# One Trainium2 core, sorted attention then four experts: early expert weights spread by GpSimd, and the head's first steps dealt to two engines

## The chip, the cores and the metric

The kernel runs on one core of a Trainium2 chip. Five engines work side by side, each with its own in-order queue: TensorE (PE; its weight loads are listed as PEld), VectorE (DVE), ScalarE (ACT), GpSimd (POOL) and SyncE (SP, which here only issues transfers). Sixteen DMA engines serve several queues. The metric is device time in microseconds (us) of one execution; the median over the runs counts.

## What is computed

```python
# attention: B, H, S, D = 4, 8, 768, 64; 8 blocks of 96 tokens
P = sort_net                                   # (B, H, 8, 8)
for _ in range(5):                             # Sinkhorn
    P = exp(P - max(P, -1)); P /= sum(P, -1) + 1e-9; P /= sum(P, -2) + 1e-9
k_sorted = einsum('bhij,bhjcd->bhicd', P, k_blocks)      # blocks mixed by P
v_sorted = einsum('bhij,bhjcd->bhicd', P, v_blocks)
attn = softmax(q_blocks @ k_sorted^T / sqrt(D))          # within each block of 96
x = (attn @ v_sorted), heads joined                      # (3072, 512)
# experts: E = 4, F = 1024
p = domain_probs / (sum(domain_probs, -1) + 1e-9)        # (3072, 4)
out = sum over e of p[:, e:e+1] * (relu(x @ w1[e]) @ w2[e])
```

Inputs are float32; the matrix products run in float16 with float32 sums.

## The kernel before

The order of the work on every engine is written out by hand: an engine runs its instructions in the order of the program text, and semaphores make it wait where it reads or overwrites what another engine has not yet finished. The expert products use a scheme of seven half-size products per block pair, so weights and hidden values are first added and subtracted (`weight_sums`, `h_sums`).

**The head (0 to some 19 us).** `sn` (32 heads by 8 by 8) is loaded, and five Sinkhorn rounds alternate between ACT (exp) and DVE. PE meanwhile multiplies a dummy block (`warm`). In the last round the column factor is multiplied in while `sn` is widened to `sn16` (L330): DVE writes the first four of the eight rows i, GpSimd the other four. `r_half(0)` (L342) multiplies `sn16` by the identity so that each factor stands on 128 partitions in PSUM (`ps_R`); `build_PI0` (L353) multiplies this by a mask and gives `PI0[0]`, the mixing matrices of the first four blocks, on DVE in two pieces of four heads. Heads are handled in two quads (`qd`), blocks in two halves (`hf`). `mix_half` (L521) mixes k or v of one quad on PE; `mixed` (L532) copies a range of blocks from PSUM; `h_w` (L548) transposes v and copies it (L553); `h_s` (L576) makes scores, with exp on ACT (L582); `h_a` (L593) applies them to v, DVE normalises (L606, L607); `h_x` (L624) transposes the result into `xT`, the experts' input, using `perm`; `group0` (L704) is the first layer of expert 0. `keep_warm` (L507) puts dummy products where PE waits. The Rs copy (L1402) takes the mixing factors of both halves out of `ps_R`. In the program the first steps stand so:

```python
mk0 = mix_half("k", 0, 0, psm, 8)       # 8 dummy products first
mixed("k", 0, mk0, 0, 2, act)
mv0 = mix_half("v", 0, 0, psa)
mixed("v", 0, mv0, 0, 2, vec)
r_half(1)
act(Rs..., Rv...)
h_s(0, 0)
mixed("k", 0, mk0, 2, 2, act)
```

Later in the head follow `mk1` and `mv1`, the mixes of the second quad. `psm` hands out two PSUM buffers in turn, so a mix waits until the buffer of two mixes before has been copied out.

**Loads.** Queries, k, v and all expert weights are float32 in DRAM and are written as float16 into SBUF; GpSimd issues these transfers, up to eight in flight, and waits for the one eight before (L113, L126, L139, L146, L183, L1456, L1475). SP issues the rest: `sn`, the probabilities twice (`p_in` at L170, with 24 tokens on each partition, and `p_own` at L171, the first 768 tokens one per partition in 16-byte pieces), the stores, and the expert weights' way: DVE divides (`spread_weights`, four steps between the Sinkhorn rounds and one later), SP writes p to DRAM (`p_dram`, L256 and L258), and `load_p` (L230) reads rows of 256 values back to all 128 partitions, as `pb`: DVE multiplies the first layer's result by `pb` where it applies the relu (L821). `load_p_one` (L241) does it for one expert of the second chunk, ahead of time. `own_weights` (L263 to L266) makes `p_sb`, the weight of expert 0 per token, which L748 uses.

**After the head.** `second_layer0` (L741, L748) is the second layer of expert 0 over batch 0; between its parts stand stages of attention (`next_stages`: `h_q_both` L288/L301, `h_w`, `h_s`, `h_a`, `h_x`). `chunk_first` (L815, L821) is the first layer of further experts in chunks of 256 tokens, `chunk` the products of the second layer (L799, L860). Batches 1 to 3 follow by a table of stages (`st_v`, `st_k`, `st_s`, `st_a`; `builds(1)` on GpSimd, L364 and L372, makes batch 1's mixing matrices), and the last five chunks use the seven-product scheme in both layers (L1153, L1166, L1296).

Of the kernel before, what the change touches and what calls it, by code (L numbers as in the profile page):

```python
# [2 lines left out]

# [7 lines left out]
F32 = mybir.dt.float32  # L11
# [7 lines left out]
def kernel(  # L19
# [67 lines left out]
    def from_spare(n):  # L87
        at = spare["at"]
        spare["at"] += n
        return Sflat[:, ds(at, n)]  # L90
# [77 lines left out]
    p_own = p_part(2 * E * NT + NT, R * E).rearrange("p (t e) -> p t e", e=E)  # L168
    own_den = p_part(2 * E * NT + NT + R * E, R).rearrange("p (t o) -> p t o", o=1)
    nc.sync.dma_start(p_in, moe_domain_probs.rearrange("(p t) e -> p t e", t=NT))  # L170
    nc.sync.dma_start(p_own, moe_domain_probs[0:S].rearrange("(t p) e -> p t e", p=P))  # L171
    load_half_queries(0)
    load_natural(0, "k", 0)

# [6 lines left out]
    for kc in range(0, NKC, 2):  # L181
# [15 lines left out]
    )  # L197

    perm = const.tile([BLK, BLK], F16, name="perm")
    nc.gpsimd.tensor_copy(  # L200
        perm.rearrange("p (c r) -> p c r", r=R), ident[0:BLK, 0:BLK].rearrange("p (r c) -> p c r", c=CP)
    )
    kTs, ETs, vs0s, wide = [], [], [], []
    for n in range(2):
        kT = const.tile([P, S + 32], F16, name=f"kT_{n}")
        nc.gpsimd.memset(kT[:, ds(S, 32)], 0.0)
        kTs.append(kT)
    for n in range(4):
        ET = const.tile([P, S + 32], F16, name=f"ET_{n}")
        nc.gpsimd.memset(ET[0:BLK, ds(S, 32)], 0.0)  # L210
        ETs.append(ET[0:BLK])
        wide.append(ET)
    for n in range(2):
        vs0 = from_spare(HB * 4 * VW)[0:BLK].rearrange("c (i s h w) -> c i s h w", i=HB, s=2, h=2)
        nc.gpsimd.memset(vs0[:, :, :, :, ds(D, 2)], 1.0)
        vs0s.append(vs0)
    vo = arena[:, ds(4 * NW + NQ + 4 * 4 * P, R * 4 * VW)].rearrange("p (r h w) -> p r h w", r=R, h=4)


# [3 lines left out]

    pbs = {}

    def load_p(b, c, es=range(E), pb=None):
        if pb is None:
            pb = moe.tile([P, E, 2 * P], F32, name=f"pb_{b}_{c}", tag="pb", bufs=1)
        n = len(es)
        nc.sync.dma_start(  # L230
            pb[:, ds(es[0], n)],
            p_dram[ds(es[0], n), ds(b * S + 2 * c * P, 2 * P)].rearrange("(o e) x -> o e x", o=1).broadcast_to(
                [P, n, 2 * P]
            ),
        )
        return pb

    def load_p_one(b, c, e):

        pb = Tt[3].rearrange("p a f x -> p (a f x)")[:, 0:4 * P].bitcast(F32)  # L240
        nc.sync.dma_start(pb, p_dram[ds(e, 1), ds(b * S + 2 * c * P, 2 * P)].broadcast_to([P, 2 * P]))  # L241
        return pb

    def spread_weights():

        nc.vector.tensor_reduce(p_den, p_in, AX.X, ALU.add)
        yield
        nc.vector.tensor_scalar(out=p_den, in0=p_den, scalar1=1e-9, scalar2=None, op0=ALU.add)
        yield
        nc.vector.reciprocal(p_den, p_den)  # L250
        yield
        nc.vector.tensor_tensor(
            p_out.rearrange("p e t -> p t e"), p_in, p_den.broadcast_to([P, NT, E]), ALU.mult
        )
        p_rows = p_dram.rearrange("e (p t) -> p e t", t=NT)
        nc.sync.dma_start(p_rows[0:S_P], p_out[0:S_P])  # L256
        pbs[(0, 0)] = load_p(0, 0)
        nc.sync.dma_start(p_rows[S_P:P], p_out[S_P:P])  # L258
        yield

    def own_weights():

        nc.vector.tensor_reduce(own_den, p_own, AX.X, ALU.add)  # L263
        nc.vector.tensor_scalar(out=own_den, in0=own_den, scalar1=1e-9, scalar2=None, op0=ALU.add)
        nc.vector.reciprocal(own_den, own_den)
        nc.vector.tensor_tensor(p_sb[:], p_own[:, :, 0:1], own_den, ALU.mult)  # L266
# [59 lines left out]
            if it:  # L326
                next(p_steps)

    for a, eng in enumerate((nc.vector, nc.gpsimd)):
        eng.tensor_tensor(  # L330
            sn16[:, ds(a * HB, HB)],
            sn[:, ds(a * HB, HB)].rearrange("g i (j o) -> g i j o", o=1).broadcast_to([GH, HB, NB, CP]),
            scol[:].rearrange("g j (i o) -> g i j o", i=1).broadcast_to([GH, HB, NB, CP]),
            ALU.mult,
        )

    ps_R = psM.tile([P, 2, 512], F32, tag="ps", name="ps_R")
    Rv = ps_R[:, :, 0:HB * GH].rearrange("p a (i g) -> p a i g", g=GH)
# [13 lines left out]
    def build_PI0(eng, a, h0, hn, src):  # L352
        eng.tensor_tensor(  # L353
            PI0[a][:, ds(h0, hn)],
            maskk[:, 0:HB * CP].rearrange("p (o i c) -> p o i c", o=1, c=CP).broadcast_to([P, hn, HB, CP]),
            src.rearrange("p g (i o) -> p g i o", o=1).broadcast_to([P, hn, HB, CP]),
            ALU.mult,
        )
# [18 lines left out]
            )  # L377

    r_half(0)
    for h0 in range(0, H, 4):  # L380
        build_PI0(nc.vector, 0, h0, 4, Rv[:, 0, :, ds(h0, 4)].rearrange("p i g -> p g i"))
    vec, act = nc.vector.tensor_copy, nc.scalar.copy


# [126 lines left out]
    def mix_half(nm, qd, hf, pool, warm_up=0):  # L511

        ps = pool([P, 1024], F32, f"ps_m{nm}_{qd}_{hf}")
        keep_warm(ps[:, 0:P], warm_up)
        tails[(nm, qd, hf)] = ps[:, 2 * R * 64:1024].bitcast(F16).rearrange("p (n x) -> p n x", n=2)
        ps = ps[:, 0:2 * R * 64].rearrange("p (s r x) -> p s r x", s=2, r=R)
        for sg in range(2):
            for r in range(R):
                for hh in range(2):
                    h = 4 * qd + 2 * sg + hh  # L520
                    nc.tensor.matmul(  # L521
                        ps[ds(D * hh, D), sg, r, :],
                        head(0, nm, h)[:, r, :],
                        PI0[hf][:, h, :, :].rearrange("p i c -> p (i c)"),
                        start=True, stop=True,
                    )
        return ps

    def mixed(nm, qd, ps, i0, n, copy):

        dst = kTs[qd][:, 0:S] if nm == "k" else vT0[qd]
        copy(  # L532
            dst.rearrange("p (i x c) -> p x i c", i=HB, c=CP)[:, :, ds(i0, n)],
            ps.rearrange("p s r (i c) -> p (s r) i c", c=CP)[:, :, ds(i0, n)],
        )
# [4 lines left out]
    def h_v(qd, hf, copy, pool=psa):  # L540
        mixed("v", qd, mix_half("v", qd, hf, pool), 0, HB, copy)
# [24 lines left out]
    def h_s(qd, qq, ps=None):  # L566

        kT, ET = kTs[qd], ETs[2 * qd + qq % 2]
        if ps is None:
            ps = psa([P, 2, 512], F32, f"ps_s0_{qd}_{qq}")  # L570
        for n in range(4):
            for hh in range(2):
                sg, i = n // 2, 2 * (qq % 2) + n % 2

                m = BLK if 2 * i + sg == 3 else P
                nc.tensor.matmul(  # L576
                    ps[0:m, hh, ds(n * BLK, BLK)],
                    kT[ds(D * hh, D), ds((2 * i + sg) * BLK, m)],
                    qT0[qd][ds(D * hh, D), sg, qq // 2, :, ds((2 * (qq % 2) + n % 2) * CP, CP)],
                    start=True, stop=True,  # L580
                )
        nc.scalar.activation(  # L582
            ET[:, 0:S].rearrange("c (h x) -> c h x", h=2), ps[0:BLK, :, 0:HS],
            AF.Exp, bias=0.0, scale=SCALE,
        )
# [248 lines left out]
    def chunk(b, c, slot, done=()):  # L834
# [9 lines left out]
                h_sums(e, 2)  # L844
        nxt = (b, c + 1) if c + 1 < R // 2 else (b + 1, 0)
        first = int(nxt[0] == 0)
        pbs[nxt] = load_p(*nxt, range(first, first + 1))
        rest = lambda: load_p(*nxt, range(first + 1, E), pbs[nxt])
        late = b == c == 1
        if not late:  # L850
            rest()

        blk = lambda kh, tok: (lambda e, f: Hb[:, homes.get(e, e), kh * KH + f, ds(tok * P, P)])
        sm = lambda n: (lambda e, f: Sb[:, n, e, ds(f * P, P)])
# [539 lines left out]
    ]  # L1394


    mk0 = mix_half("k", 0, 0, psm, 8)
    mixed("k", 0, mk0, 0, 2, act)
    mv0 = mix_half("v", 0, 0, psa)
    mixed("v", 0, mv0, 0, 2, vec)  # L1400
    r_half(1)
    act(Rs.rearrange("p g (a i) -> p a g i", a=2), Rv.rearrange("p a i g -> p a g i"))  # L1402
    h_s(0, 0)
    mixed("k", 0, mk0, 2, 2, act)
    load_half_queries(1)
    load_w2(0, 2)
    build_PI0(nc.gpsimd, 1, 0, H, Rs[:, 0:H, HB:NB])
# [24 lines left out]
    even01()  # L1432
    w11(vec)
    group0(0, 1, 1, [0, 1])
    own_weights()
    ps_s11 = ps_a10
    h_s(1, 1, ps_s11)
    evacuate00 = group0(0, 1, 0, [2, 3], True)
# [9 lines left out]
    group0(1, 1, 0, [2, 3])  # L1448
    h_v(0, 1, vec)
    h_v(1, 1, vec)  # L1450
    group0(1, 1, 1, [2, 3])


# [15 lines left out]
            build_PI(nc.gpsimd, n, "k")  # L1469

    load_w2(1)
    load_w2(2)
    load_w1(3)
    def load_w2_part(e, d):
# [22 lines left out]
                f(*args)  # L1497

    second_layer0(0, next_stages)
    load_queries(1, range(2))  # L1500
    load_natural(1, "v", 0, 2, lambda: load_w2_part(3, DH))
    load_natural(1, "k", 0, 2)
    load_natural(1, "v", 1)
    load_natural(1, "k", 1)
    chunk_first(0, 0, [1, 2], 1, next_stages)
    pb_1 = load_p_one(0, 1, 1)
    h_sums(1, 4)
    for w in range(1, 5):
        h_sums(2, w)
# [3 lines left out]
    second_layer0(1, lambda: next(sums2, None))  # L1513
    sums0 = weight_sums(0, nc.vector)
    homes[1] = 0
    chunk_first(0, 1, [1], 1, next_stages, lambda e: pb_1.rearrange("p (o x) -> p o x", o=1))
    homes.clear()


# [27 lines left out]
    for g in range(G0 + 1, GN, 2):  # L1547
        last_second(g, last_first(g))
        last_second(g + 1, upper=True)
# [1 line left out]
_INS = ['q', 'k', 'v', 'sort_net', 'moe_domain_probs', 'moe_w1', 'moe_w2']  # L1551
_OUTS = [((3072, 512), 'float32')]
# [25 lines left out]
```

## Time and profile before

| | |
|---|---|
| median of 3 runs | 358.14 us (358.12 to 358.28) |
| the profiled execution | 358.21 us |
| its span, first to last instruction | 356.3 us |
| PE, DVE, ACT, POOL busy | 350.4, 277.5, 170.1, 137.6 us |
| moved by DMA | 40.26 MB in 74762 packets |
| granted TensorE clock | 1.00 throughout |

The profiled execution is one of the program's; what it takes beside its span (1.9 us) lies before the first and after the last instruction. A row of a group names the line, the engine, the operation, what is written and read, and the busy time; in the chain, each row is a start, a length and what ran. A busy PE is not PE at its peak, since products overlap.

### The profile page before, as it was taken

The numbers are of one execution on the slowest core, as the hardware profiler recorded it, in microseconds if no ns is written. First come the engines' busy times: TensorE is split into PE (matmuls) and PEld (weight loads), VectorE is DVE, ScalarE is ACT, GpSimd is POOL, SyncE is SP. The second block draws the span as 40 slices with busy tenths as digits, with TensorE's granted clock in tenths as the row PEclk, the third lists the DMA queues.
The fourth block names the chain that finished last, engine by engine and source line by source line (L and its number), as shares of the span: only waits on it lengthen the run. The fifth ranks groups of instructions, "written<-read, shape, count | busy, mean of one in ns | idle before, by whom it ended". The sixth has DMA issues, their size and how long they took to land.

```text
span 356.3 us, 9511 instructions
## 1 busy us (share of the span) xinstructions
PE 350.4 (98%) x3948; PEld 305.5 (86%) x3948; DVE 277.5 (78%) x555; ACT 170.1 (48%) x302; POOL 137.6 (39%) x154
## 2 busy tenths in 40 slices
PE   8899999999999999999999999999999999999996
PEld 8686857888888888988899888888888888888886
DVE  5766787779798687778879988896678886588963
ACT  2653330452425445368847259830288611598301
POOL 8766112466022420000626318840068800188400
PEclk9999999999999999999999999999999999999999
DMA  8999999999999999743995410005200014100021
GB/s 104 203 205 230 212 209 194 207 195 167 195 180 166 195 116 203 138 88 44 180 205 91 107 74 0 2 1 136 78 26 3 2 37 141 62 0 2 0 75 46
DMA packets 74762, 40.26 MB, mean 113 GB/s; under 512 B 41568, under 2 KB 70496, under 8 KB 74720
## 3 DMA queue, kind: packets, MB, share of 16 engines
q0 software_dynamic: 38720, 19.93, 43.2%
q1 hardware_dynamic: 35856, 19.67, 27.2%
q8 instruction: 31, 0.51, 0.6%
q14 instruction: 11, 0.09, 0.1%
q10 hardware_dynamic: 144, 0.07, 0.1%
HBM read 41.88 MB, written 6.34 MB: 135 GB/s over the span
## 4 chain that ended last, share of the span: by engine, by line
PE 95%; DVE 3%; issue 0%; DMA 0%; ACT 0%; DVEq 0%
PE ps_h L815 18%; PE ps_Q L1296 18%; PE ps_p L799 12%; PE ps_X L1153 10%; PE ps_Z L1153 7%; PE ps_Q L1153 7%; PE ps_Z L1296 6%; PE ps_h L704 3%; PE ps_o L741 3%; PE ps_p L860 3%; PE ps_a L479 2%; PE ps_s L444 2%; PE ps_k L425 1%; PE ps_v L391 1%; PE ps_mv L521 1%; PE ps_a L593 0%
## 5 line engine op out<-in xcount | busy, mean ns | idle before, releaser
L815 PE MATMUL ps_h<-xT,w 128*128 128x256 f16 x576 | 67.5, 273 | 0.0
L815 PEld LDWEIGHTS <-w 128*128 128x128 f16 x576 | 55.2, 98 | 7.3
L821 DVE SCALAR_TENSOR_TENSOR Hb<-ps_h,pb 128x1024 f16<-128x1024 f32 x34 | 41.5, 1223 | 17.8 <-PE ps_h L815 17.6
L1153 PEld LDWEIGHTS <-w 128*128 128x128 f16 x480 | 43.6, 98 | 4.7
L1166 POOL TENSOR_TENSOR arena<-tmp,pb 128x512 f16<-128x512 f32 x12 | 15.2, 1276 | 65.7 <-PE ps_Z L1153 49.8
L1296 PEld LDWEIGHTS <-Hb 128*128 128x128 f16 x320 | 31.1, 98 | 3.5
L1165 ACT ACTIVATE tmp<-tmp 128x512 f32<-128x512 f32 x46 | 29.0, 632 | 3.9 <-DVE tmp L1203 3.9
L1296 PEld LDWEIGHTS <-Sb 128*128 128x128 f16 x304 | 28.2, 98 | 3.0
L1153 PEld LDWEIGHTS <-arena 128*128 128x128 f16 x312 | 27.7, 98 | 2.8
L451 ACT ACTIVATE ET<-ps_s 96x768 f16<-96x768 f32 x24 | 18.1, 802 | 25.2 <-PE ps_s L444 25.0
L434 ACT CAST kT<-ps_k 64x384 f16<-64x384 f32 x48 | 22.7, 473 | 13.3 <-PE ps_k L425 12.3
L126 POOL DMA_DIRECT2D arena<-in_q_dram x24 | 19.9, 842 | 20.8 <-DMA q_ring<-arena 17.7
L1153 PE MATMUL ps_X<-ET,arena 128*128 128x256 f16 x168 | 25.2, 272 | 0.0
L1296 PE MATMUL ps_Q<-w,Hb 128*128 128x256 f16 x192 | 24.6, 273 | 0.0
L799 PEld LDWEIGHTS <-Hb 128*128 128x128 f16 x232 | 21.9, 98 | 3.0
L1159 DVE SCALAR_TENSOR_TENSOR Hb<-ps_X,pb 128x512 f16<-128x512 f32 x27 | 18.7, 692 | 7.0 <-PE ps_X L1153 7.0
L1173 ACT COPY ps_X<-ps_Z 128x512 f32<-128x512 f32 x27 | 15.4, 571 | 17.8 <-PE ps_Z L1153 17.8
L1153 PE MATMUL ps_Z<-xT,w 128*128 128x256 f16 (+1 forms) x176 | 22.5, 258 | 0.0
L785 DVE TENSOR_TENSOR Sb<-Hb 128x512 f16<-128x512 f16 x33 | 20.6, 646 | 0.0
L1180 ACT COPY tmp<-ps_X 128x512 f32<-128x512 f32 x26 | 15.2, 586 | 9.2 <-PE ps_X L1153 6.6
L1159 DVE SCALAR_TENSOR_TENSOR Hb<-ps_Z,pb 128x512 f16<-128x512 f32 x27 | 18.4, 683 | 1.3 <-PE ps_Z L1153 1.3
L1203 DVE TENSOR_TENSOR tmp<-ps_Q,tmp 128x512 f32<-128x512 f32 x26 | 17.7, 683 | 0.8 <-PE ps_Q L1153 0.8
(270 smaller groups left out, 744.3 us busy)
## 6 DMA issues: line engine op xcount, KB each, us to landing
w<-in_moe_w_dram POOLq DMA_DIRECT2D x4, 1024.0 KB, 27.2
w<-in_moe_w_dram POOLq DMA_DIRECT2D x6, 512.0 KB, 19.7
arena<-in_k_dram POOLq DMA_DIRECT2D x7, 384.0 KB, 7.6
arena<-in_v_dram POOLq DMA_DIRECT2D x7, 384.0 KB, 8.1
vs<-arena SPq DMA_DIRECT2D x36, 66.0 KB, 5.3
arena<-in_q_dram POOLq DMA_DIRECT2D x24, 96.0 KB, 7.5
out_dram<-ob SPq DMA_DIRECT2D x9, 256.0 KB, 2.0
pb<-p_dram SPq DMA_DIRECT2D x4, 512.0 KB, 5.8
```

Of the source, the lines that this page charges most:

```text
L126: nc.gpsimd.dma_start(t[:, h // 2, :, h % 2, :], q[b, h].rearrange("(t p) d -> p t d", p=P))
L434: nc.scalar.copy(kT[ds(D * hh, D), r], pk[ds(D * r, D), hh].rearrange("p a (i c) -> p a i c", c=CP),)
L451: nc.scalar.activation(ETs[2 * (pr % 2) + hh][:, 0:S].rearrange("c (a x) -> c a x", a=2), pss[hh][0:BLK, :, 0:HS], AF.Exp, bias=0.0, scale ...
L785: tt(sm[0], blk(0, 1), blk(1, 1), ALU.add)
L799: nc.tensor.matmul(ps, lhs(e, f), Ts[e][rhs][:, f, :], start=(first and e == es[0] and f == 0), stop=(done and e == es[-1] and f == KH - 1 ...
L815: nc.tensor.matmul(ps[:, f, :], w1sb[e][:, kc, ds((4 * g + f) * P, P)], xT[:, kc, ds(2 * c * P, 2 * P)], start=(kc == 0), stop=(kc == NKC ...
L821: nc.vector.scalar_tensor_tensor(out=Hb[:, homes.get(e, e), ds(4 * g, 4), :], in0=ps[:], scalar=0.0, op0=ALU.max, in1=weights(e).broadcast ...
L1153: nc.tensor.matmul(dst[:, ds(f * cols, cols)], a[lhs][:, k, ds((f0 + f) * P, P)], t[rhs][:, k, :], start=(first and f == 0 and k == 0), st ...
L1159: nc.vector.scalar_tensor_tensor(out=home(i, j), in0=src.rearrange("p (f x) -> p f x", f=m), scalar=0.0, op0=ALU.max, in1=weight(j).broadc ...
L1165: nc.scalar.activation(src, src, AF.Relu, bias=0.0, scale=1.0)
L1203: tt(t12, Q, u2, ALU.add)
L1296: nc.tensor.matmul(ps, lhs(e, f), Ts[e][rhs][:, f, part], start=(first and e == 0 and f == 0), stop=(e == E - 1 and f == KH - 1), skip_gro ...
```

## The change

It has two parts.

*Expert weights of the first two chunks.* For the first chunk SP now loads only the rows of experts 1 to 3 into partition 0 of the tile (`load_rows`), and GpSimd copies partition 0 to all partitions (`spread`, a `partition_broadcast`). That operation needs another library of GpSimd code, loaded in the program after `load_w2(1)`; the usual one is loaded again at the end. `load_p_one` does the same for its row and stands earlier. The second chunk's tile is loaded for experts 2 and 3 only. `p_own` is loaded after p's first write to DRAM, and `own_weights` stands later, after the last mix of v (`h_v(1, 1, vec)`).

*The head.* Row 3 of `sn16` moves from DVE to GpSimd. `PI0[0]` is built in three pieces. The first two blocks of k and of v are copied one by ACT and one by DVE, and k's other two in two pieces. `h_s(0, 0)` stands ahead of `r_half(1)`, the Rs copy moves to DVE, four dummy products go, and the constants (`perm`, zeros, ones) are written by GpSimd after its part of `sn16`.

```diff
-    nc.sync.dma_start(p_own, moe_domain_probs[0:S].rearrange("(t p) e -> p t e", p=P))
     load_half_queries(0)
...
+    def fill_constants():
+        for kT in kTs:
+            nc.gpsimd.memset(kT[:, ds(S, 32)], 0.0)
+        for ET in ETs:
+            nc.gpsimd.memset(ET[:, ds(S, 32)], 0.0)
+        for vs0 in vs0s:
+            nc.gpsimd.memset(vs0[:, :, :, :, ds(D, 2)], 1.0)
+        nc.gpsimd.tensor_copy(
+            perm.rearrange("p (c r) -> p c r", r=R), ident[0:BLK, 0:BLK].rearrange("p (r c) -> p c r", c=CP)
+        )
...
     def load_p_one(b, c, e):
         pb = Tt[3].rearrange("p a f x -> p (a f x)")[:, 0:4 * P].bitcast(F32)
-        nc.sync.dma_start(pb, p_dram[ds(e, 1), ds(b * S + 2 * c * P, 2 * P)].broadcast_to([P, 2 * P]))
+        pb = pb.rearrange("p (o x) -> p o x", o=1)
+        load_rows(pb, b, c, [e])
+        spread(pb)
         return pb
+
+    def load_rows(dst, b, c, es):
+        nc.sync.dma_start(
+            dst[0:1], p_dram[ds(es[0], len(es)), ds(b * S + 2 * c * P, 2 * P)].rearrange("(o e) x -> o e x", o=1)
+        )
+
+    def spread(dst):
+        nc.gpsimd.partition_broadcast(dst, dst[0:1])
...
         nc.sync.dma_start(p_rows[0:S_P], p_out[0:S_P])
-        pbs[(0, 0)] = load_p(0, 0)
+        nc.sync.dma_start(p_own, moe_domain_probs[0:S].rearrange("(t p) e -> p t e", p=P))
+        pbs[(0, 0)] = pb_tile(0, 0)
+        load_rows(pbs[(0, 0)][:, 1:E], 0, 0, range(1, E))
         nc.sync.dma_start(p_rows[S_P:P], p_out[S_P:P])
...
-    for a, eng in enumerate((nc.vector, nc.gpsimd)):
+    for eng, i0, n in ((nc.vector, 0, HB - 1), (nc.gpsimd, HB - 1, 1), (nc.gpsimd, HB, HB)):
         eng.tensor_tensor(
...
+    fill_constants()
...
-    for h0 in range(0, H, 4):
-        build_PI0(nc.vector, 0, h0, 4, Rv[:, 0, :, ds(h0, 4)].rearrange("p i g -> p g i"))
+    for h0, n in ((0, 2), (2, 2), (4, 4)):
+        build_PI0(nc.vector, 0, h0, n, Rv[:, 0, :, ds(h0, n)].rearrange("p i g -> p g i"))
...
-        pbs[nxt] = load_p(*nxt, range(first, first + 1))
-        rest = lambda: load_p(*nxt, range(first + 1, E), pbs[nxt])
         late = b == c == 1
-        if not late:
-            rest()
+        if nxt == (0, 1):
+            pbs[nxt] = load_p(*nxt, range(2, E))
+        else:
+            pbs[nxt] = load_p(*nxt, range(first, first + 1))
+            rest = lambda: load_p(*nxt, range(first + 1, E), pbs[nxt])
+            if not late:
+                rest()
...
-    mk0 = mix_half("k", 0, 0, psm, 8)
-    mixed("k", 0, mk0, 0, 2, act)
+    mk0 = mix_half("k", 0, 0, psm, 4)
+    mixed("k", 0, mk0, 0, 1, act)
+    mixed("k", 0, mk0, 1, 1, vec)
     mv0 = mix_half("v", 0, 0, psa)
-    mixed("v", 0, mv0, 0, 2, vec)
+    mixed("v", 0, mv0, 0, 1, vec)
+    mixed("v", 0, mv0, 1, 1, act)
+    h_s(0, 0)
     r_half(1)
-    act(Rs.rearrange("p g (a i) -> p a g i", a=2), Rv.rearrange("p a i g -> p a g i"))
-    h_s(0, 0)
-    mixed("k", 0, mk0, 2, 2, act)
+    vec(Rs.rearrange("p g (a i) -> p a g i", a=2), Rv.rearrange("p a i g -> p a g i"))
+    for i in (2, 3):
+        mixed("k", 0, mk0, i, 1, act)
...
     group0(0, 1, 1, [0, 1])
-    own_weights()
...
     h_v(1, 1, vec)
+    own_weights()
     group0(1, 1, 1, [2, 3])
...
     load_w2(1)
+    nc.gpsimd.load_library(library_config.all_libraries[10])
+    spread(pbs[(0, 0)][:, 1:E])
     load_w2(2)
...
     second_layer0(0, next_stages)
+    pb_1 = load_p_one(0, 1, 1)
     load_queries(1, range(2))
...
     chunk_first(0, 0, [1, 2], 1, next_stages)
-    pb_1 = load_p_one(0, 1, 1)
...
+    nc.gpsimd.load_library(library_config.standard)
```

More of the change, by code (lines that the diff above doesn't have):

```diff
@@ L5 @@
 import concourse.tile as tile
-from concourse import mybir
+from concourse import library_config, mybir
 from concourse.bass import ds
@@ L199 @@
     perm = const.tile([BLK, BLK], F16, name="perm")
-    nc.gpsimd.tensor_copy(
-        perm.rearrange("p (c r) -> p c r", r=R), ident[0:BLK, 0:BLK].rearrange("p (r c) -> p c r", c=CP)
-    )
     kTs, ETs, vs0s, wide = [], [], [], []
     for n in range(2):
-        kT = const.tile([P, S + 32], F16, name=f"kT_{n}")
-        nc.gpsimd.memset(kT[:, ds(S, 32)], 0.0)
-        kTs.append(kT)
+        kTs.append(const.tile([P, S + 32], F16, name=f"kT_{n}"))
     for n in range(4):
         ET = const.tile([P, S + 32], F16, name=f"ET_{n}")
-        nc.gpsimd.memset(ET[0:BLK, ds(S, 32)], 0.0)
         ETs.append(ET[0:BLK])
@@ L213 @@
     for n in range(2):
-        vs0 = from_spare(HB * 4 * VW)[0:BLK].rearrange("c (i s h w) -> c i s h w", i=HB, s=2, h=2)
-        nc.gpsimd.memset(vs0[:, :, :, :, ds(D, 2)], 1.0)
-        vs0s.append(vs0)
+        vs0s.append(from_spare(HB * 4 * VW)[0:BLK].rearrange("c (i s h w) -> c i s h w", i=HB, s=2, h=2))
+    def fill_constants():
[8 more added lines that the diff above has]
+        )
     vo = arena[:, ds(4 * NW + NQ + 4 * 4 * P, R * 4 * VW)].rearrange("p (r h w) -> p r h w", r=R, h=4)
@@ L224, with pb_tile @@
     pbs = {}
+    def pb_tile(b, c):
+        return moe.tile([P, E, 2 * P], F32, name=f"pb_{b}_{c}", tag="pb", bufs=1)
     def load_p(b, c, es=range(E), pb=None):
         if pb is None:
-            pb = moe.tile([P, E, 2 * P], F32, name=f"pb_{b}_{c}", tag="pb", bufs=1)
+            pb = pb_tile(b, c)
         n = len(es)
@@ L327 @@
                 next(p_steps)
-    for a, eng in enumerate((nc.vector, nc.gpsimd)):
+    for eng, i0, n in ((nc.vector, 0, HB - 1), (nc.gpsimd, HB - 1, 1), (nc.gpsimd, HB, HB)):
         eng.tensor_tensor(
-            sn16[:, ds(a * HB, HB)],
-            sn[:, ds(a * HB, HB)].rearrange("g i (j o) -> g i j o", o=1).broadcast_to([GH, HB, NB, CP]),
-            scol[:].rearrange("g j (i o) -> g i j o", i=1).broadcast_to([GH, HB, NB, CP]),
+            sn16[:, ds(i0, n)],
+            sn[:, ds(i0, n)].rearrange("g i (j o) -> g i j o", o=1).broadcast_to([GH, n, NB, CP]),
+            scol[:].rearrange("g j (i o) -> g i j o", i=1).broadcast_to([GH, n, NB, CP]),
             ALU.mult,
         )
+    fill_constants()
     ps_R = psM.tile([P, 2, 512], F32, tag="ps", name="ps_R")
@@ L1515 @@
     homes[1] = 0
-    chunk_first(0, 1, [1], 1, next_stages, lambda e: pb_1.rearrange("p (o x) -> p o x", o=1))
+    chunk_first(0, 1, [1], 1, next_stages, lambda e: pb_1)
     homes.clear()
```

## The prediction

> **What bounds the kernel now.** I read the page first (busy shares, chain), then the chain in order of time, the table by stage, the timeline of the head, and the landing times of single transfers.
>
> ```profile
> PE 350.4 (98%) x3948; PEld 305.5 (86%) x3948; DVE 277.5 (78%) x555; ACT 170.1 (48%) x302; POOL 137.6 (39%) x154
> ...
> PE 95%; DVE 3%; issue 0%; DMA 0%; ACT 0%; DVEq 0%
> ```
>
> TensorE carries 95% of the chain that ends last, DMA none of it. In the table by stage PE is busy for 7.00 of 7.00 us in 24:31 and 99.97 of 100.00 in 80:180, so later stages have nothing to give. What can be gained lies before 18.8 us; what can be lost lies wherever a cover ends.
>
> The head, from the chain between 16.1 and 18.9 us:
>
> ```profile
> 16.08 0.13 PE ps_s L576 x6
> 16.21 0.52 PE ps_mv L521 x24
> 16.73 0.02 issue
> 16.76 0.57 DVE Sb L532
> 17.32 0.04 issue
> 17.37 0.44 PE ps_mv L548 x4
> 17.81 0.03 issue
> 17.83 0.02 DVEq L553
> 17.86 0.04 issue
> 17.90 0.43 DVE Sb L553
> 18.33 0.04 issue
> 18.37 0.40 PE ps_a L593 x8
> 18.77 0.17 PE ps_h L704 x2
> ```
>
> Here PE and DVE hand work to each other; from 18.77 the first layer fills PE. This last hand-over starts with mixing the second quad's v (`mv1`). The timeline shows when that v arrives:
>
> ```profile
> 16.15 0.57 PE L521 MATMUL ps_mv<-Sb,arena 128*64 128x64 f16 x24
> ...
> 16.39 0.75 POOL L146 DMA_DIRECT2D w<-in_moe_w_dram  x1 [1.18 <-DMA arena<-in_v_dram]
> ```
>
> ```profile
> L113 POOL DMA_DIRECT2D arena<-in_v_dram x1: 760/760/760, 5.6 to 5.6; - x1
> ...
> DMA to landing us min/median/max: 10.5/10.5/10.5
> ```
>
> Issued at 5.62 with 10.5 us to land: v is there at 16.1, `mv1` starts at 16.15. An earlier ready head meets that gate.
>
> **The change, part by part.** The profiled execution took 358.21 us, its span 356.3, so 1.9 us lie around it; the median of the runs is 358.14. I sum against 358.21 and move the result by -0.07.
>
> *Head.* Fits from rows: DVE 0.16 us + 1.04 ns a column (L532: 0.557 us for 384, 0.958 for 768); ACT 0.14 + 0.88 (0.479 and 0.817); Pool's two-input f32 0.16 + 2.2 (0.72 for 256 at L970, 1.27 for 512 at L1166).
>
> - sn16: DVE writes 384 columns, not 512: 0.68 to 0.55. Pool's single row is 0.44 and can start at 10.87, since perm and the memsets (10.44 to 11.27) move behind it: ready at 11.31, DVE at 11.41. Gain 0.13.
> - PI0: the first piece is two heads, 0.29 for 0.42. Gain 0.13; pieces two and three (another 0.6) run behind PE's first twelve matmuls. Four fewer warming matmuls (8 in 0.55) make room; the four removed were cover only.
> - k halves: one piece each on ACT (0.31) and DVE (0.36) in parallel for 0.48 in one. v halves likewise: DVE's piece 0.36 for 0.56. Before, v's first half was ready at 13.99; now mk ends at 12.77, mv at 13.14, DVE's k piece at 13.15, its v piece at 13.53. Gain up to there 0.46.
> - h_s(0,0) goes ahead of r_half(1) on PE, and the Rs copy from ACT (0.37) to DVE (0.16 + 256 x 1.04 ns = 0.42). It falls at 13.75 to 14.17, in DVE's wait for the transposes (0.59 idle before L553); queued behind it are L553 and `mk1`, which needs the PSUM buffer that Rs frees (14.23 instead of 14.40). ACT pays one fixed part more for k's last two pieces and ends `mk1`'s copy at 15.68 for 15.85; that frees `mv1`'s buffer.
> - So PE could start `mv1` at 15.73. But v lands at 16.10. Of the 0.42 nothing comes through unless v lands sooner. What could bring it: p_own's load (768 pieces of 16 bytes, 1.66 to 5.57) leaves this stretch. It is one of the small HW-queue loads beside two query loads that had landed by 6.4, while k and v followed until 16.1 at some 200 GB/s. Bounds for v: 0 to 0.5 us sooner; I take 0.1, since the transfers that it ran beside are not the ones that end last. Head: -0.1 us (0 to -0.42).
> - A moved constant: the ones, zeros and perm (0.83 us on Pool) now end at 13.3; their readers start at 14.6 (h_a), 15.4 (h_s(0,1)), 16.2 (h_x). Half-queries 1 are issued at 13.3 for 12.40; needed at 28.7, landed at 23.2. Nothing.
>
> The row that could undo the 0.13: DVE and Pool now work on sn16 at the same time. Before, they overlap from 11.23 to 11.54 and Pool's op takes 1.23 us, no more than L1166's 1.27 for as many columns. But at 331 us three L785 sums (0.41 each when Pool is quiet) take 3.02 us beside L1166. The Trainium skill (SBUF — State Buffer, section "SBUF: two separate sides") says that a DVE op with two SBUF inputs and a GpSimd op that reads SBUF lock each other out for the whole instruction. The trace agrees at 331 us and does not at 11.2 us. By the rule the row would be ready at 11.85, v's half at 13.96, `mv1` at 16.2, and the sum would be 358.2 instead of 358.0.
>
> *Expert weights.* Removed from the DMA engines: four rows to 128 partitions (512 KB, 25.5 to 35.9), one row (128 KB, 26.6 to 39.2) and two of the four rows at 63.8 (256 KB). 640 KB at some 205 GB/s: the weights behind them land 3.1 us sooner. PE waited for none of them (DMA 0%): 0 us, but a reserve.
> Added on SP, in order: the first write of p (19.99), p_own, the rows (after the write, landed at 25.5), the second write, the one row. On Pool: a library load at 22.6 (w2(1)'s issue ends at 22.59), a broadcast of 768 words and one of 256. Queued behind the first: w2(2), w1(3), half of w2(3), four builds, batch 1's loads; DVE's L821 waits for it. Its own length: nearest is a Pool copy (maskv, 0.30 us for 128 columns; so 1.0), at most L1166's pace (1.9); 1.0. The rows: 3.5 to 5.5 us after 25.5, as the small write took (5.5): 30 to 31. The library load is in no row. From below ACT's table load, 1.28 us; from above, if it waits for the transfers in flight, w2(1)'s landing (21.7 + 25.1 = 46.8). Nearest are SP's transfers of that stretch, 5.5 to 12.6 us to land: Pool free at 28 to 35, broadcast done by 31.5 to 36.2.
> Needed by: L821 starts at 38.79, and with two PSUM buffers PE first waits at 41.16, so it may start at 39.9. Cover 3.7 us or more. The software queue stays fed by w2(1) until 43.7 (46.8 less 3.1), so late issues of w2(2) and after cost nothing. The builds end near 41 and are used at 63.7. The second broadcast's row lands near 33 and holds up nothing that isn't in that queue anyway. Later Pool products run from the other library; taken at the same 1.27 us. The closing reload follows Pool's last op (333.8), 22 us before the end. 0 us.
> The Trainium skill (GPSIMD Engine Reference, 2.1 Instruction dispatch) gives about 6 us for the first call after a load; no row here shows one. By that Pool is free near 28.6, and the sum is the same.
>
> *own_weights* (0.70 us of DVE at 21.13 to 21.92, off the chain) moves to 28.64, into DVE's 0.96 us wait before L301; it ends at 29.4, L301 starts at 29.61. That needs p_own by 28.5. Issued at 20.4; the 128-piece write took 5.5, and 768 pieces took 2.1 longer than 128 at the start (3.9 against 1.8): landed at 28.0. Bounds 24.3 (3.9) to 32.6 (12.2, the second write). 0 us.
>
> Sum: -0.1. 358.21 - 0.1 - 0.07 = **358.0 us**, own range 357.6 to 358.6.
>
> **The rivals.**
> 1. *Pool is held too long* (slower). The library load waits for transfers in flight: released at 43.7, broadcast done at 44.7, L821 starts 4.9 us after the latest harmless time (39.9): 363.0. It decides once load and broadcast end after 39.9. For: Pool's queue is in order and the load stands amid a saturated stretch (DMA share 1.19 to 1.28). Against: 3.7 us of cover at the nearest rows' worst. Chance 0.25, spread from 358.9 to 364.
> 2. *p_own is late* (slower): at 30.5, DVE's L301 ends at 31.9, ACT's second half (which starts behind it, 30.20 after 30.17) at 32.8 instead of 31.0; PE's spare there is 0.2. 1.7 us: 359.8. Decides from p_own after 28.5. For: HW-queue transfers of this stretch took up to 12.6 us. Chance 0.13.
> 3. *The head's gain comes through* (faster): v lands 0.5 sooner and the waits of 0.10 and 0.11 us at 19.49 and 31.32 close as well: 0.46 + 0.2 = 0.66, and with pieces a little cheaper than fitted 0.9: 357.3 to 357.5. For: p_own's pieces do run beside the first loads. Against: v's own queue ran at 200 GB/s after them. Chance 0.20.
>
> **How the numbers follow.** The sum: 0.42. No change here means within 0.2% (0.72 us), about what a measurement of this kernel can tell. Faster: 0.15 of rival 3 and 0.01 of the sum, 0.16. Slower: rival 1 (0.25), rival 2 (0.12), 0.01 of the sum, 0.38. The rest, 0.46, is no change. The range reaches from rival 3 to half of rival 1: 357.3 to 361.5, with about 0.05 left out below and 0.13 above.
>
> **What would show it.** Right: r_half's first matmul at about 11.46, v's first half at 13.5, `mv1` still at 16.0 to 16.1 behind v's landing; no 512 KB pb load; w2(1) landing near 43.7; L821's first at 38.7, released by PE; own_weights near 28.5 without a wait. Wrong: L821 or PE's L815 idle with Pool as releaser (rival 1), a DVE gap released by a DMA before L263 (rival 2), `mv1` before 15.9 (rival 3), or L1166 longer than 1.53 us, two of which would fill the 3.06 us step of the last products.

## The result

The changed kernel takes 364.02 us (median of 6 runs, 361.46 to 365.49); before, in the same session, 358.33 (6 runs, 358.12 to 358.90). The ratio is 1.0152, 95% interval 1.0128 to 1.0177: slower by 5.7 us, where 358.0 was forecast and a range of 357.3 to 361.5. The profiled execution took 363.61 us, its span 361.6, against 358.21 and 356.3: 5.4 us to be found. It moved 39.47 MB instead of 40.26.

The page of after, busy times and the chain's engines. A DMA now holds 3% of the chain:

```profile
PE 351.7 (97%) x3944; PEld 306.2 (85%) x3944; DVE 278.6 (77%) x558; ACT 169.8 (47%) x303; POOL 139.8 (39%) x157
...
PE 91%; DVE 4%; DMA 3%; issue 1%; ACT 1%; SPq 0%; DVEq 0%
```

The chain of after in order of time (start, length, what ran) names it:

```profile
20.31 0.30 SPq L272
20.61 0.04 issue
20.66 10.87 DMA T<-in_moe_domain_probs_dram
31.53 0.02 issue
31.55 0.19 DVE T L281
...
32.68 1.06 DVE p_sb L284
33.74 0.06 DVE Sb L319
33.80 0.33 issue
34.13 0.68 DVE Sb L572
34.81 0.04 issue
34.85 0.73 PE ps_s L595 x16
35.59 1.82 PE ps_o L760 x4
...
42.17 1.85 PE ps_h L834 x16
```

(Lines moved by some 15 to 20: L281 to L284 are `own_weights`, L319 the copies of `h_q_both`, L572 the copy of `h_w`, L595 `h_s`, L760 and L834 the products that were L741 and L815.) This is the load of `p_own`: issued at 20.66, landed at 31.53. `own_weights` waits for it, the two copies are queued behind it on DVE, and PE waits for the second. The timeline of after shows both waits in brackets, with who ended them:

```profile
31.34 1.05 POOL L258 PARTITION_BROADCAST pb<-pb  x1 [8.84 <-DMA pb<-p_dram]
31.55 0.18 DVE L281 TENSOR_REDUCE T<-T 128x6 f32<-128x24 f32 x1 [2.63 <-DMA T<-in_moe_domain_probs_dram]
31.76 0.66 DVE L282 TENSOR_SCALAR T<-T 128x6 f32<-128x6 f32 x1
...
32.68 1.06 DVE L284 TENSOR_TENSOR p_sb<-T 128x6 f32<-128x6 f32 x1
...
34.85 0.73 PE L595 MATMUL ps_s<-Sb,kT 64*128 64x96 f16 x16 [3.57 <-DVE Sb L572]
```

The wait is followed by a slower clock. In the table by stage (PE busy, PEld, DVE, ACT, POOL, then the granted clock, DMA share, GB/s) the stretch behind the gap has 0.57:

```profile
31.00:35.00 4.00, 0.43 (x10) 0.24 (x9) 3.35 (x7) 0.76 (x1) 3.65 (x5) 1.00 1.30 208
35.00:39.00 4.00, 4.00 (x32) 2.27 (x27) 1.15 (x2) 1.54 (x3) 4.00 (x4) 0.57 1.24 208
```

From the scores behind the gap to the first product of the next chunk PE takes 42.17 - 34.85 = 7.32 us; before it took 36.90 - 31.00 = 5.90. So: head 0.28 (below), gap 3.57, the slow stretch 1.42, together 5.27 of the 5.4 us; the first product of the chunk starts at 42.17 instead of 36.90.

The head of after, from sn16 to the first transposes of v (L567):

```profile
10.84 0.55 DVE L348 TENSOR_TENSOR sn<-sn,scol 32x384 f16<-32x384 f32 x1
10.89 1.77 POOL L348 TENSOR_TENSOR sn<-sn,scol 32x128 f16<-32x128 f32 x2
...
12.96 0.32 ACT L551 CAST kT<-ps_mk 128x192 f16<-128x192 f32 x1 [2.00 <-PE ps_mk L540]
13.31 0.36 DVE L551 CAST kT<-ps_mk 128x192 f16<-128x192 f32 x1 [0.49 <-ACT kT L551]
13.58 0.35 DVE L551 CAST Sb<-ps_mv 128x192 f16<-128x192 f32 x1
...
13.96 0.32 ACT L551 CAST Sb<-ps_mv 128x192 f16<-128x192 f32 x1 [0.69 <-DVE Sb L551]
```

The pieces that were dealt to ACT and DVE run one behind the other: DVE waits 0.49 us for ACT's piece of k, ACT 0.69 for DVE's piece of v. v's first half is ready at 14.28, not at 13.53 as forecast and not at 13.99 as before. It stays so to the end of the head, and v's landing isn't the gate any more (issued at 5.8, landed by 15.4):

```profile
L113 POOL DMA_DIRECT2D arena<-in_v_dram x2: 785/794/802, 4.3 to 5.8; - x2
...
DMA to landing us min/median/max: 7.2/8.3/9.6
```

```profile
16.21 0.28 PE ps_s L595 x8
16.49 0.52 PE ps_mv L540 x24
...
18.65 0.41 PE ps_a L612 x8
```

`mv1` starts at 16.49 (before 16.21 in the chain), the last step of the head at 18.65 (before 18.37): 0.28 us later.

### The profile page after: what moved, and what is told of

It is laid out like the page before. It is cut to its first block, busy times and chain, and to the rows that moved or that the text cites. A ratio compares the mean times of both kernels' runs of the same rounds, so it can differ in the third digit from the quotient of the medians.

```text
span 361.6 us, 9514 instructions
## 1 busy us (share of the span) xinstructions
PE 351.7 (97%) x3944; PEld 306.2 (85%) x3944; DVE 278.6 (77%) x558; ACT 169.8 (47%) x303; POOL 139.8 (39%) x157
## 2 busy tenths in 40 slices
DMA packets 73954, 39.47 MB, mean 109 GB/s; under 512 B 41524, under 2 KB 69688, under 8 KB 73912
## 4 chain that ended last, share of the span: by engine, by line
PE 91%; DVE 4%; DMA 3%; issue 1%; ACT 1%; SPq 0%; DVEq 0%
PE ps_h L834 18%; PE ps_Q L1318 17%; PE ps_p L818 12%; PE ps_X L1175 10%; PE ps_Z L1175 7%; PE ps_Q L1175 7%; PE ps_Z L1318 6%; DMA T<-in_moe_domain_probs_dram 3%; PE ps_o L760 3%; PE ps_p L882 3%; PE ps_a L498 2%; PE ps_s L463 2%; PE ps_h L723 1%; PE ps_k L444 1%; PE ps_v L410 1%
## 5 line engine op out<-in xcount | busy, mean ns | idle before, releaser
L834 PE MATMUL ps_h<-xT,w 128*128 128x256 f16 x576 | 67.5, 273 | 0.0
L834 PEld LDWEIGHTS <-w 128*128 128x128 f16 x576 | 55.2, 98 | 7.3
L1195 ACT COPY ps_X<-ps_Z 128x512 f32<-128x512 f32 x27 | 15.4, 571 | 17.8 <-PE ps_Z L1175 17.8
```

What stands on the lines that cost most here:

```text
L834: nc.tensor.matmul(ps[:, f, :], w1sb[e][:, kc, ds((4 * g + f) * P, P)], xT[:, kc, ds(2 * c * P, 2 * P)], start=(kc == 0), stop=(kc == NKC ...
```

## The experiments

Ratios are to before in the same session, whose medians lay at 358.2 to 358.4.

**1. p_own's load back at the start, everything else as changed.**

```diff
     nc.sync.dma_start(p_in, ...)
+    nc.sync.dma_start(p_own, moe_domain_probs[0:S].rearrange("(t p) e -> p t e", p=P))
...
-        nc.sync.dma_start(p_own, ...)        # in spread_weights
```

> The changed kernel with one line put back: p_own is loaded at the start again (own_weights stays late). Theory A (p_own's 768 small pieces, loaded amid the weights, land at 31.5 us and hold DVE, then PE): no DVE wait before own_weights, no 3.6 us PE gap at 31.3, no slow clock behind it; what is left is the head's 0.3 us: 358.6 us. Theory B (Pool is held by the library load and the broadcast, and that makes the loss): the gap stays, 362 to 364 us.

Measured: 358.75 us (12 runs), ratio 1.0017 (0.9996 to 1.0037). p_own lands 3.9 us after its issue, DVE's wait and PE's gap are gone. The place of this one load is 5.3 of the 5.7 us.

**2. Before, with p_own and own_weights moved as in the change, nothing else.**

> The kernel before with only p_own's load moved behind the first write of p, and own_weights moved as in the change. No library, no broadcast, old head. Theory A: p_own lands at 30 to 32 us, DVE waits for it, PE has a gap of about 3 us and then runs some us at a lower clock: 361.5 to 363 us. Theory B: no change, 358.3 us.

Measured: 362.3 us (6 runs), ratio 1.0098 (1.0072 to 1.0125). So the late load alone makes some 4 of the 5.7 us. The timeline has the same two waits, without any broadcast:

```profile
33.45 0.18 DVE L263 TENSOR_REDUCE T<-T 128x6 f32<-128x24 f32 x1 [3.63 <-DMA T<-in_moe_domain_probs_dram]
33.67 0.17 DVE L264 TENSOR_SCALAR T<-T 128x6 f32<-128x6 f32 x1
...
34.10 0.17 DVE L266 TENSOR_TENSOR p_sb<-T 128x6 f32<-128x6 f32 x1
...
35.38 0.60 PE L576 MATMUL ps_s<-Sb,kT 64*128 64x96 f16 x16 [3.19 <-DVE Sb L553]
```

Here the load took 11.9 us and the clock behind the gap was 0.60. The four small ops take 0.82 us together; in after 2.19 (31.55 to 33.74), L282 beside the broadcast and L284 beside GpSimd's next weight issues (L146, L139). That adds up to 1.4 us to PE's wait in after. What holds L284 is open: beside the same kind of issue the same op took 0.17 us in experiment 8 (at 22.47).

**3. Half of p_own's pieces early, half late** (384 pieces of 16 bytes each).

```diff
+    nc.sync.dma_start(p_own[:, 0:3], moe_domain_probs[0:S // 2]...)     # at the start
-        nc.sync.dma_start(p_own, moe_domain_probs[0:S]...)
+        nc.sync.dma_start(p_own[:, 3:R], moe_domain_probs[S // 2:S]...)  # behind p's first write
```

> The changed kernel with p_own's load in two: 384 pieces at the start, 384 at the late place. If the number of small pieces sets the landing, it falls from 10.9 us after issue by half of the time the pieces ran (6.6 us) to 7.5 us: landed at 28 to 28.5, DVE waits 0 to 0.5 us, total 358.8 to 360 us. If the place in the queue sets it, it lands at 31 us as before and the total stays at 362 to 365 us.

Measured: 360.36 us (10 runs, 358.77 to 362.18), ratio 1.005 (1.0032 to 1.0068). In the profiled execution (358.77) the late half landed 7.0 us after its issue, at 27.95, and no engine waited for it:

```profile
DMA to landing us min/median/max: 7.0/7.0/7.0
```

At the same place in the queue, half of the pieces saves some 4 to 5 of 10.9 to 12.2 us: their number sets most of the landing. The median lies above the forecast range all the same. The profiled run is the shortest of the ten; six of the others had a mean clock of 0.995 or less (359.22 to 362.18), the four at full clock a median of 359.0. What the longer runs waited for wasn't profiled.

**4. own_weights moved on, ahead of its first use.**

```diff
-    own_weights()                      # behind h_v(1, 1, vec)
...
+            if col == 0:
+                own_weights()          # in second_layer0, ahead of the first multiply by p_sb
             nc.vector.tensor_scalar(
                 out=oaccs[col][:], in0=ps, scalar1=p_sb[:, col], ...
```

> The changed kernel with own_weights moved further back, to just ahead of its first reader. p_own lands as late as before, but DVE's copies for the scores stand ahead of the wait. Theory A: no 3.6 us PE gap; DVE waits at 31 to 33 us with one output tile in reserve, so PE waits 0 to 1.5 us later on: 358.7 to 360.5 us. Theory B: the loss stays, 362 to 364 us.

Measured: 360.72 us (6 runs), ratio 1.0071 (1.0054 to 1.0087). The load still took 11.8 us, but PE's gap is 1.31 us: the copies of `h_q_both` and `h_w` no longer stand behind the waiting instruction. Where the wait stands costs 3.3 of the 5.7 us; what is left lies just above theory A's range.

**5. PE's gap filled with 60 dummy products**, into a PSUM bank that nobody reads.

```diff
             if col == 0:
+                ahead.append(psm([P, 2, 512], F32, "ps_o_1"))
+                keep_warm(ahead[0][:, 1, 0:P], 60)
```

> The changed kernel with 60 dummy products (about 3.3 us) on PE where it waits for p_own's consumers, into the unused bank of the next output tile. Theory A with the clock as its second half: the wait itself stays (p_own still lands at 31 to 33 us), but PE stays busy, the granted clock stays 1.00 after it, and about 1.3 us come back: 362.5 to 363 us for 364.0. If the clock behind the gap cost nothing: 364 us or more.

Measured: 363.47 us (4 runs), ratio 1.0147 (1.0133 to 1.0162). The clock holds:

```profile
35.00:39.00 4.00, 3.22 (x41) 1.97 (x41) 2.39 (x5) 2.30 (x3) 4.00 (x6) 1.00 1.24 207
```

From the scores to the chunk's first product PE takes 41.43 - 35.78 = 5.65 us, against 7.25 in after by the same rows of the timeline (34.85 to 42.10): the slow clock was worth 1.6 us. Only 0.4 to 0.6 of it shows in the times; in this profile p_own landed at 33.24, 1.7 us later than in after, so the wait itself was longer.

**6. The weights' part alone, with p_own and own_weights in their old places.**

> The kernel before with the weights' part alone, p_own and own_weights at their old places. Theory A: weights land 3 us sooner, PE waits for none of them, 358.1 to 358.4 us. Theory B: Pool's hold reaches DVE's relu (L821 in the kernel before), 360 us or more.

Measured: 358.6 us (12 runs), ratio 1.0002 (0.9991 to 1.0012). Library, broadcasts and 0.79 MB less traffic change nothing that can be measured.

**7. The head's part alone.**

> The kernel before with the head's part alone. Theory C (Pool's row is stretched beside DVE, and the two engines copy the halves one after the other, not side by side): first layer starts 0.2 to 0.3 us later, 358.5 to 358.7 us. Theory D (the head is faster but meets v's landing, as forecast): 358.0 to 358.3 us.

Measured: 359.6 us (11 runs), ratio 1.0032 (1.0018 to 1.0045): more than any theory gave. In its profiled execution the clock falls in the head:

```profile
15.00:19.00 4.00, 4.00 (x83) 3.28 (x81) 2.60 (x7) 2.60 (x6) 3.27 (x4) 0.50 1.24 205
```

**8. The head's part with the four dummy products back.**

```diff
-    mk0 = mix_half("k", 0, 0, psm, 4)
+    mk0 = mix_half("k", 0, 0, psm, 8)
```

> The head's part alone on the kernel before, but with all 8 dummy products kept ahead of the first mix. If the loss of the head alone (359.6 against 358.35) is mostly PE's clock (0.50 between 15 and 19 us in its profile), it shrinks to the 0.3 us of the later hand-over: 358.5 to 358.8 us, clock 1.00 in the head. If it is the copies and Pool's row themselves: 359.3 to 359.6 us.

Measured: 359.34 us (11 runs), ratio 1.0028 (1.0016 to 1.0040). In the profile:

```profile
15.00:19.00 4.00, 3.69 (x99) 3.12 (x100) 3.08 (x7) 3.46 (x8) 3.19 (x4) 1.00 1.24 205
```

Nine of the 11 runs had a mean clock of 0.999 or more, median 358.96; of experiment 7's runs 6 of 11, median 359.0. So the clock explains at most the upper half of experiment 7 and not the other 0.6 us: the loss lies in the head's own steps, the second reading.

**9. v's second block copied into a tile of its own** (experiment 8 otherwise).

```diff
+    vx = const.tile([P, 2 * BLK], F16, name="vx")
...
+        if (nm, qd, n) == ("v", 0, 1) and i0 == 1:
+            copy(vx..., ps...[:, :, ds(i0, n)])
+            return
```

> The head part with eight dummy products (as in e8_head_warm8), but v's second block is copied by ACT into a tile of its own instead of into the tile that DVE writes its first block to. Theory T (the second engine waits because both write one tile): ACT's piece of v no longer waits 0.69 us for DVE's; it starts as soon as ACT's piece of k is done (13.55 in that profile), the transposes start about 0.35 us sooner than in e8_head_warm8, and the time is 358.6 to 358.7 us (e8: 359.34 as a median, about 358.96 at a full clock). Theory S (two engines that read one PSUM tile go one after the other): the wait on DVE's copy stays and the time is 358.9 to 359.0.

Measured: 359.03 us (10 runs), ratio 1.0033 (1.0012 to 1.0054); ACT still waits 0.69 us for DVE's copy, as theory S has it.

**10. The same for k and v, and sn16 dealt as before** (four rows each).

> Before plus the head part alone, with eight dummy products, four rows of sn16 on GpSimd as before, and the second blocks of k and v copied into tiles of their own. Theory T: no copy waits for the other engine's; k's pieces end together, v's some 0.35 us behind them, the first transposes start 0.6 us sooner than in e8_head_warm8, and the time is 357.9 to 358.2 us, set by v's landing (15.1 to 17.3 us in the profiles so far). Theory S: 358.9.

Measured: 358.8 us (12 runs), ratio 1.0012 (1.0001 to 1.0023). No written tile is shared any more, and yet:

```profile
13.28 0.32 ACT L545 CAST kT<-ps_mk 128x192 f16<-128x192 f32 x1 [1.99 <-PE ps_mk L528]
14.29 0.32 ACT L539 CAST vx<-ps_mv 128x192 f16<-128x192 f32 x1 [0.69 <-DVE Sb L545]
```

```profile
13.63 0.36 DVE L539 CAST kT<-ps_mk 128x192 f16<-128x192 f32 x1 [0.51 <-ACT kT L545]
13.91 0.35 DVE L545 CAST Sb<-ps_mv 128x192 f16<-128x192 f32 x1
```

Theory T falls. What the two pieces still share is the PSUM tile that they read, and in the trace each second copy carries a semaphore wait on the other engine: it is the program that puts them in turn. Whether the chip could read both pieces at once is shown by no run here, and no run gives the pieces two PSUM tiles. Two engines do copy side by side where the PSUM tiles differ: before, ACT reads `ps_mk` from 14.68 and DVE reads `ps_mv` from 14.92 to 15.46, with 0.54 us, its usual length. The kernel before had the rule in a row of its own, where the two halves of one tile `ps_q` go to two engines (`h_q_both`):

```profile
29.61 0.56 DVE L301 COPY Sb<-ps_q 128x768 f16<-128x768 f16 x1 [0.96 <-PE ps_q L288]
...
30.20 0.80 ACT L301 COPY Sb<-ps_q 128x768 f16<-128x768 f16 x1 [1.43 <-DVE Sb L301]
```

**11. Whole copies and the order of before; the row of sn16 and PI0's three pieces stay.**

> The head part with eight dummy products, but the copies of k and v, the Rs copy on ACT and the order of r_half and h_s as before; what is left of the head part is GpSimd's fifth row of sn16, the later constants and PI0 in three pieces. Theory A (the dealt copies and their order cost the head's 0.6 us): 358.2 to 358.4 us (the third piece of PI0 gains 0.13, the row loses 0.05). Theory B (the row and the pieces of PI0 cost it): 358.8 to 359.0.

Measured: 358.61 us (12 runs), ratio 1.0005 (0.9996 to 1.0014). The median lies between the two theories; the profiled execution has the wait of 0.53 us near 193 that the last section shows.

**12. PI0's three pieces alone.**

> Before with one edit: PI0 of the first four blocks is built in three pieces (two, two and four heads). Theory A (the piece that PE waits for first is 0.13 us shorter, nothing else changes, and the transfers of weights in the middle leave room): the first mix of k starts 0.13 us sooner after sn16 than in before, 358.1 to 358.3 us where before has 358.2 to 358.35. Theory B (a head that is ahead of before gives it back at the weight transfer near 193 us, as the profile of e11_whole_copies has it): 358.4 to 358.6, with PE waiting there for a DMA.

Measured: 358.31 us (12 runs, 357.86 to 362.81) against 358.39; ratio of the means 1.0018 (0.9994 to 1.0042), raised by two long runs. Inconclusive in time; the profiled execution took 357.97 us without a wait near 193. In the traces the head's edits add up. From the start of sn16 on DVE to the first transposes of v, each from the timeline of one execution:

| kernel | us |
|---|---|
| before | 14.04 - 10.86 = 3.18 |
| PI0's pieces (12) | 14.16 - 11.07 = 3.09 |
| and the row (11) | 14.22 - 11.09 = 3.13 |
| and the dealt copies, in their new order (8) | 14.60 - 11.08 = 3.52 |
| the same without the row (10) | 14.66 - 11.19 = 3.47 |
| after (four dummies fewer) | 14.33 - 10.84 = 3.49 |

So PI0's pieces gain 0.09, the row costs 0.04, the dealt copies with their order 0.39. That the head alone loses 0.6 in time and not 0.3 has one more step in experiments 7 to 10: near 25 us PE waits 0.23 to 0.25 us for `xsl`, a wait that neither before nor after has. There DVE starts to normalise only when PE's next mix of k is done, at 23.97 in experiment 8, though the product that it reads ended at 23.46; in experiment 1, where own_weights stands later, it starts behind its own product:

```profile
23.97 0.20 DVE L611 RECIPROCAL rz<-ps_a 96x8 f32<-96x8 f32 x1 [1.33 <-PE ps_mk L526]
```

```profile
24.23 0.20 DVE L625 RECIPROCAL rz<-ps_a 96x8 f32<-96x8 f32 x1 [1.96 <-PE ps_a L612]
```

So the two parts of the change are not independent, and the head costs less within the whole change (some 0.4 us in experiment 1) than alone (1.25 in experiment 7). Why the one program waits for the mix is open.

**13. The whole change, mended:** p_own early, eight dummies, sn16 dealt as before, own tiles for the second blocks.

> The whole change with four edits: p_own is loaded at the start again, eight dummy products stand ahead of the first mix, GpSimd takes four rows of sn16 instead of five, and the second blocks of k and v are copied into tiles of their own. Theory T (shared destination tiles, the late p_own and the clock are the whole loss): v's first blocks are ready some 0.6 us sooner than in the change, mv1 waits for v's landing, and the time is 357.9 to 358.3 us, no more than before's 358.35. Theory S (two engines that read one PSUM tile go one after the other): 358.7 to 359.0. If the weights' part costs something of its own beside these, this run lies above e12_head_mended by it.

Measured: 358.42 us (12 runs), ratio 1.001 (0.9997 to 1.0024), between the two theories; in its profile the second copies still wait 0.52 and 0.69 us. No kernel of these was faster than before beyond the noise.

## Why the prediction was wrong

- *"landed at 28.0 ... 0 us"* is the step that failed. The place, the engine and the mechanism were those of rival 2 (0.13), and its bounds (24.3 to 32.6) held the measured 31.53; the value chosen in between did not. It added 2.1 us, the price of 768 pieces at the quiet start, to a write of 128 pieces in the busy stretch. In the busy stretch the pieces themselves are slow: 10.9 to 12.2 us for all of them in four profiles, 7.0 for half.
- The price of rival 2 was too small as well. By its rule 31.53 would cost 2.7 us; it cost 5.0. Missing were the clock behind a PE gap of over 3 us (1.4 to 1.6 us) and the stretching of own_weights (0.76 us expected, 28.64 to 29.4; 2.19 measured); part of these falls into the 0.28 by which the head was late anyway.
- *"the four removed were cover only"*: probably wrong. With four dummies 14 of 23 runs of experiments 1 and 7 kept a mean clock of 0.999, with eight 63 of 69 (experiments 8 to 13). But the copies differ among these kernels too, a mean over the whole execution doesn't say where the clock fell (in the profile of experiment 8 it fell at 194 to 198 us, behind another wait), and experiments 7 and 8, which differ in the dummies alone, have 6 and 9 of 11: too few to settle it.
- *k and v halves "in parallel"*: wrong. Of the 0.46 to be gained 0.20 was theirs; they lost 0.39, and with all edits v's transposes began 0.31 later (3.49 for 3.18). The two pieces come from one PSUM tile and are taken in turn. Rival 2 names the row that showed it, ACT's half that "starts behind it, 30.20 after 30.17", but the head's sum didn't use it.
- *sn16, gain 0.13*: the row was to take 0.44 and be ready at 11.31. It took 0.76 beside DVE (10.89 to 11.65), and a fourth product waits for it. By the rule of the Trainium skill (SBUF — State Buffer, section "SBUF: two separate sides"), that GpSimd and DVE lock each other out, it would have been ready at 11.85; the traces bear the lock out, and the row ends 0.26 us behind DVE's op instead of the 0.44 that the forecast added. That the trace "does not" agree at 11.2 us was a misreading: the 1.23 us there were compared with another op's 1.27, while the same op alone takes 1.04 (last section). One small DVE op of own_weights points the same way: 0.17 us alone, 0.66 beside the broadcast (L282).
- *PI0, gain 0.13*: 0.09 in the trace.
- Right: the broadcast of 768 words takes 1.05 us (1.0), L821's cover holds, w2(1) lands at 43.5 (43.7), the other products on GpSimd keep 1.27 us, the weights' part is worth 0 us. The main rival, a library load that holds GpSimd, did not happen: GpSimd waited until 31.34 for the rows, not for the library. So its own length doesn't show; it lies within the 8.84 us that GpSimd stood idle. The Trainium skill (GPSIMD Engine Reference, section 2.1 Instruction dispatch) has some 6 us for the first call after a load; no run here can show it. One slip changed nothing: of the rows loaded at 63.8 one went, not two.
- `mv1` was forecast to wait for v; v landed earlier (15.4) and the late copies were the gate.

The forecast set its widest rival on the part that looked strange, the library, and took the smallest edit, a load moved by 19 us, from the wrong row.

## What to carry to other kernels

A small load of many tiny pieces belongs where the DMA queues are quiet; moved into a saturated stretch it took 11 to 12 us instead of 4. Put the instruction that waits for a load directly ahead of its first use, since whatever is queued behind it on that engine waits as well, and count the slow clock after a long PE gap into its price. Two engines that copy parts of one PSUM tile were taken in turn in this program, those that copy different tiles ran side by side; so different tiles are what to try, which no run here did for these copies.

## What the hardware showed that was not expected

- A gap of 3.2 to 3.6 us on PE was followed by 4 us at 0.57 to 0.60 of the clock, and dummy products in the gap kept it at 1.00.
- In the profiled execution of experiment 13, PE paused for 0.89 us at 13.9 with nothing that the profile shows for it ("issue"), and the clock fell to 0.50 in 15 to 19 us; that execution took 360.93 us, the other eleven 358.18 to 358.86. Experiment 9 has such a pause at the same place, of 0.65 us, and kept 1.00. What causes the pause is open.
- GpSimd's part of sn16 waits for DVE's. Where the two overlap, in 14 of the 15 profiles, it ends a fixed time behind DVE's op, 0.91 us with four rows and 0.26 with the single row, though they overlap by 0.32 us in before and by 0.63 in experiment 10; where it starts behind DVE's op, in experiment 6 (third row), its four rows take 1.04 and not 1.23 as before:

```profile
10.86 0.68 DVE L330 TENSOR_TENSOR sn<-sn,scol 32x512 f16<-32x512 f32 x1
11.23 1.23 POOL L330 TENSOR_TENSOR sn<-sn,scol 32x512 f16<-32x512 f32 x1
```

```profile
11.81 1.04 POOL L348 TENSOR_TENSOR sn<-sn,scol 32x512 f16<-32x512 f32 x1
```

- One transfer of weights has little room: it is issued at 184 to 186 us, and PE wants it some 8 us later. It took 5.8 us before; in the profile of experiment 11 it took 8.7 and PE waited 0.53 us, in that of experiment 8 10.5 and 2.75 (an execution of 363.53 us):

```profile
193.28 0.62 PE L1158 MATMUL ps_Q<-xT,w 128*128 128x128 f16 x8 [0.53 <-DMA w<-arena]
```

That may be part of the spread of the runs, against which 0.1 us gained in the head can't be seen in a median; only these two profiles show it.
